# V's main weights: one transfer, or four in the order in which they are multiplied

## The chip, the cores and the metric

The kernel runs on one core of a Trainium2 chip. The metric is the time of one execution in microseconds of device time. Below, TensorE is the matrix engine (PE in the profile, PEld its weight loads), VectorE is DVE, ScalarE is ACT, GpSimd is POOL, and SyncE is SP, which here only issues transfers; SPq and ACTq are the queues of transfers that SP and ScalarE issue.

## The reference

The input x has 2048 rows of 576. It is normalised (layernorm), and two branches read the result: attention with 32 heads of 18 and a sliding window of 256, and a gated MLP with 4608 hidden units. Their outputs are added to x.

```python
def reference(A_x, A_wqkv, A_wo, B_x, B_w1, B_w3, B_w2):
    x = A_x                                   # 1 x 2048 x 576
    xn = _layernorm(x, axis=-1)
    return x + _A_ref(xn, A_wqkv, A_wo) + _B_ref(xn, B_w1, B_w3, B_w2)

def _A_ref(x, wqkv, wo):                      # H = 32, Dh = 18, W = 256
    q, k, v = ((x @ wqkv).reshape(B, S, 3, H, Dh)).transpose(2, 0, 3, 1, 4)
    scores = q k^T * Dh ** -0.5, masked to 0 <= i - j < W
    return softmax(scores) v, heads side by side, @ wo

def _B_ref(x, w1, w3, w2):
    return (silu(x @ w1) * (x @ w3)) @ w2
```

All tensors are bfloat16. The columns 1152 to 1727 of `wqkv` are V's weights: 576 rows, 576 columns.

## The kernel before

**The work.** The 2048 rows are taken in four chunks of 512 (`NC`, `CH`), each of four tiles of 128 rows (`TB`). For each chunk the kernel computes Q, K and V, then the MLP's hidden units with the attention between them, then the output. The normalised rows lie transposed in `xnT`, with the 576 inputs on the partitions: four blocks `kd` of 128 and a last one of 64, which stands on both halves of the partitions.

**Two halves of the array.** Almost every multiplication uses 64 of the 128 rows of the array (`tile_position`), and two run side by side: one on partitions 0 to 63, one on partitions 64 to 127. A projection is cut into two parts (`proj_part`). In part 0 the upper half of the partitions gives column half 0 and the lower half column half 1; in part 1 it is the other way round, so that each output is the sum over all rows. For V a column half is `HD` = 288 columns wide. So V's part 0 reads, of the tile `wv`, partitions 0 to 63 in columns 0 to 287 and partitions 64 to 127 in columns 288 to 575; part 1 reads the rest, and the block `kd` = 4 as well, which is loaded on its own (key `wvd`, line 901).

**The order.** Every operation is added by hand to one list, with the engine that runs it and the keys that it reads and writes. From the keys the program derives the waits: a reader of a loaded tile waits until that load's semaphore has reached the count of its writers. Each engine runs its operations in the order in which they were added. Transfers are added to SP's list or to ScalarE's, and are issued in that order.

**The start.** ScalarE's queue loads x tiles 1 to 3, and SP's queue x tile 0. Behind it SP issues `wv` (line 897, one transfer of four blocks to 128 partitions), `wvd` (901, two), and the weights of Q and K into a staging area that is laid over the tile `pt` (927 and 931, six transfers, semaphores `wqk0`, `wqkd`, `wqk1`). Then come the first six transfers of the MLP's weights (`load_part`, 330), which wait for the second tile's copy of `xnT`. TensorE runs fillers (921, 909, 915) until x tile 0 is normalised; it transposes it (429), ScalarE copies it to `xnT` (442, 448), and V's part 0 of tile 0 starts (500). V's tiles follow as x tiles 1 to 3 become ready; ScalarE and VectorE move V's results to `va` (549, 551). GpSimd and VectorE deal the weights of Q and K from `pt` to `wp` (952, `deal`), and Q's projection (500 with `wp`) comes behind V's last tile. SP then issues `xnS` (463), a copy of `xnT` with the halves of the partitions swapped, which the MLP's first layer (768) reads beside `xnT`.

```python
        early = kind == "v" and c == 0
        order = range(4 + part if kind == "v" else 5 - part)
        for n in order:
            for r in range(2):
                x = r ^ part
                kd, r0 = (4 if n == 4 else n), 64 * r
```

Of the kernel before, what the change touches and what calls it, by code (L numbers as in the profile page):

```python
# [44 lines left out]
class _Prog:  # L45
# [13 lines left out]
    def add(self, eng, fn, r=(), w=(), j=(), dma=None, after=()):  # L59
        deps = []  # L60
        for k in r:
            deps += self.bufs[k].writers
        for k in w:
            g = self.bufs.get(k)
            if g is not None:
                deps += g.ahead(eng)
        for k in j:
            g = self.bufs[k].before
            if g is not None:
                deps += g.ahead(eng)  # L70
        op = _Op(eng, fn, deps + list(after), dma)
        op.after = tuple(after)
        self.n[eng] += 1
        op.pos = self.n[eng]
        if dma is not None:
            self.dma_count[dma] = self.dma_count.get(dma, 0) + 16
            op.cnt = self.dma_count[dma]
        for k in r:
            self.bufs[k].readers.append(op)
        for k in w:  # L80
            self.bufs[k] = _Gen([op], self.bufs.get(k))
        for k in j:
            self.bufs[k].writers.append(op)
        for k in w:
            if self.bufs[k].before is not None:
                self.bufs[k].before.before = None
        self.ops.append(op)
        return op
# [76 lines left out]
def bass_parallel_sum__sliding_block__glu_gated_swiglu__prompt_kernel(  # L165
# [11 lines left out]
    D = A_x.shape[2]  # L177
# [11 lines left out]
    HD = D // 2  # L189
# [6 lines left out]
    add = P.add  # L196

    with ExitStack() as es:

        def sb(name, shape, dtype=dt.bfloat16):  # L200
            return es.enter_context(nc.sbuf_tensor(name, shape, dtype))
# [14 lines left out]
        xnT = sb("xnT", [128, 2, 5, CH])  # L216
        xnS = sb("xnS", [128, 4, CH])
        wv = sb("wv", [128, 5, D])
# [248 lines left out]
        def xk(c):  # L467
            return [("xnT", c % 2, tt) for tt in range(TB)]


        def pair_of(c, i):

            return (((0, 1), (2, 3), (8, 4), (5, 6)) if c == 0 else ((8, 0), (1, 2), (3, 4), (5, 6)))[i]

        def proj_part(c, what, banks, part, behind=()):

            kind, i = what
            last = []
# [6 lines that stand above are left out]
                    rows = slice(r0, r0 + 64)  # L485
                    out_ = PS[:, banks[x], :]
                    if kind == "q":
                        t = pair_of(c, i)[x]
                        st, mv = wp[rows, kd, t, :], xnT[rows, c % 2, kd, :]
                        keys = [("wp", t)] + xk(c)  # L490
                    elif kind == "8":
                        out_ = PS[:, banks[x], 0:CH // 2]
                        st, mv = wp[rows, kd, i, :], xnT[rows, c % 2, kd, x * (CH // 2):(x + 1) * (CH // 2)]
                        keys = [("wp", i)] + xk(c)
                    else:
                        out_ = PS[:, banks[x], 0:HD]
                        st, mv = xnT[rows, c % 2, kd, i * 128:(i + 1) * 128], wv[rows, kd, x * HD:(x + 1) * HD]
                        keys = ["wvd" if kd == 4 else "wv", (("xnTb" if kd // 2 else "xnTa"), i) if early and kd < 4 else ("xnT", c % 2, i)]
                    first = part == 0 and n == 0
                    op = add("pe", lambda e, out_=out_, st=st, mv=mv, n=n, r0=r0, first=first: e.matmul(  # L500
                        out_, st, mv, start=first, stop=(part == 1 and n == order[-1]), tile_position=(r0, 0)),
                        r=keys, after=behind if n == 0 else (), **{"w" if first else "j": [("ps", banks[x])]})
                    if n == order[-1]:
                        last.append(op)
            return last
# [23 lines left out]
        def proj_end(later=None, late=None):  # L529
            if pend:  # L530
                c, what, banks, last = pend.pop()
                proj_part(c, what, banks, 1, last)
                proj_out(c, what, banks, later, late)
                return what

        def proj_begin(c, what, banks=None):
            banks = banks or job()
            last = proj_part(c, what, banks, 0)
            got = proj_end()
            pend.append((c, what, banks, last))  # L540
            return got
# [348 lines left out]
                    p2_mm(ACC[half][tt] if turn is None or turn >= 0 else ACC[0][turn + 2], half, r, *args)  # L890


        xslot = {}
        for t in range(TB):
            xslot[t] = load_x(t, "act" if t else "sp")
        add("act", lambda e: e.preload_act_table_set("sqrt_and_others"))
        add("sp", lambda e: e.dma_start(
            wv[:, 0:4, :], A_wqkv[0:512, 2 * D:3 * D].rearrange("(kd p) f -> p kd f", p=128)),
            w=["wv"], dma="wv")
        for p in range(2):  # L900
            add("sp", lambda e, p=p: e.dma_start(
                wv[64 * p:64 * p + 64, 4, (1 - p) * HD:(2 - p) * HD],
# [21 lines left out]
        for h in range(2):  # L924
            for n in range(2):
# [3 lines left out]
                    dma=f"wqk{h}", **{"j" if n else "w": [f"wqk{h}"]})  # L929
# [119 lines left out]
        for c in range(NC):  # L1049
# [21 lines left out]
            early = [("h", n) for n in range(4 if c == 0 else 0, NHP)]  # L1071
# [111 lines left out]
            for u in range(NF):  # L1183
# [44 lines left out]
                if c == 0 and u == 13:  # L1228
                    for t in range(4):
# [3 lines left out]
                            dma="wo", **{"j" if t else "w": ["wo"]})  # L1233
                if c == 0 and u == 18:
                    rows = A_wo[0:4 * Dh, :].rearrange("(n d) f -> n d f", d=Dh)
                    add("sp", lambda e: e.dma_start(wo[126:128, 0:4, :], rows[:, 0:2, :].rearrange("n d f -> d n f")),
                        j=["wo"], dma="wo")
                    for p in range(2):
                        add("sp", lambda e, p=p: e.dma_start(wo[64 * p:64 * p + 64, 4, :], rows[:, 2:Dh, :]),
                            j=["wo"], dma="wo")  # L1240
# [64 lines left out]
```

## Time and profile before

| | us |
|---|---|
| median of 3 runs | 555.67 (555.06 to 555.78) |
| the profiled execution | 555.25 |
| its span in the profile | 553.5 |
| TensorE busy | 549.7 (99%) |
| VectorE / ScalarE / GpSimd busy | 313.3 / 259.3 / 210.8 |
| HBM read and written | 71.29 MB and 2.36 MB |

The span runs from the first instruction to the last; the 1.75 us between span and time lie around it. A row of the timeline gives the start in us from the span's start, the time taken by the group, the engine, the line of the kernel, the operation, the tile written and the tiles read, and the number of instructions; in brackets stands the idle time of the engine before it and what ended it. For a transfer the time taken is that of its issue on the queue's engine; the DMA view gives the time from issue to landing, and over a window the number of packets, the megabytes and the mean rate. A row of the chain of waits gives a start, a duration, and the work that the end waited for in that stretch.

### The profile page before, as it was taken

What the parts mean: (1) busy time and instruction counts of PE and PEld (TensorE: products, weight loads), DVE (VectorE), ACT (ScalarE), POOL (GpSimd) and SP (SyncE); (2) the same over time, 40 slices, a digit from 0 to 9 for tenths busy, and PEclk for the clock granted to TensorE, in tenths of its full rate; (3) what the DMA queues carried; (4) which work ended last, traced back from release to release, by engine and by line L of the source; (5) the groups of instructions that cost most, each with busy time, mean ns of one, the idle gap of its engine ahead of it and who ended that gap; (6) DMA issues with size and microseconds to landing.
All of it is one profiled execution on the core that took longest, in us unless ns stands there. A gap on an engine that the chain in (4) does not pass through costs nothing.

```text
span 553.5 us, 18356 instructions
## 1 busy us (share of the span) xinstructions
PE 549.7 (99%) x8072; PEld 338.6 (61%) x8072; DVE 313.3 (57%) x587; ACT 259.3 (47%) x365; POOL 210.8 (38%) x380
## 2 busy tenths in 40 slices
PE   8999999999999999999999999999999999999998
PEld 5677544777555544477765454557776545445776
DVE  7476797710468886651056988655105567866311
ACT  7457776000288567700037857760005784775000
POOL 4324675400047456530005745643001553663100
DMA  9997799476577953756746885466673773541750
GB/s 246 204 199 173 199 202 229 129 202 181 141 144 145 188 134 92 186 141 194 185 111 140 173 157 146 124 143 164 183 181 85 139 172 102 152 117 44 194 151 23
DMA packets 128038, 86.00 MB, mean 155 GB/s; under 512 B 35702, under 2 KB 125646, under 8 KB 127958
## 3 DMA queue, kind: packets, MB, share of 16 engines
q1 hardware_dynamic: 89138, 62.80, 49.9%
q10 hardware_dynamic: 38820, 22.02, 15.7%
q8 instruction: 63, 1.03, 0.8%
q14 instruction: 17, 0.14, 0.1%
HBM read 71.29 MB, written 2.36 MB: 133 GB/s over the span
## 4 chain that ended last, share of the span: by engine, by line
PE 99%; DMA 1%; DVE 0%; issue 0%; ACT 0%
PE ps L768 51%; PE ps L839 29%; PE ps L500 10%; PE ps L630 6%; PE ps L698 3%; DMA xp<-in_A_x_dram 1%; PE ps L429 0%; DVE stats L396 0%; DVE xn L414 0%; ACT sd L369 0%; DVE ofin L861 0%; PE ps L915 0%; DVE mv L399 0%; DVE rstd L374 0%
## 5 line engine op out<-in xcount | busy, mean ns | idle before, releaser
L768 PE MATMUL ps<-xnT,w 64*128 64x512 bf16 x1400 | 186.4, 376 | 0.0
L768 PE MATMUL ps<-xnS,w 64*128 64x512 bf16 x1120 | 152.4, 376 | 0.0
L839 PE MATMUL ps<-w,hT 64*128 64x288 bf16 x2292 | 143.7, 282 | 0.0
L783 DVE SCALAR_TENSOR_TENSOR gs<-th,ps 128x512 bf16<-128x512 bf16 x144 | 97.9, 680 | 78.8 <-ACT th L777 78.0
L839 PEld LDWEIGHTS ps<-w,hT 64*128 64x128 bf16 x2292 | 112.3, 94 | 29.5 <-issue 0.2
L777 ACT ACTIVATE th<-ps 128x512 bf16<-128x512 f32 x144 | 85.6, 594 | 60.6 <-PE ps L768 59.7
L768 PEld LDWEIGHTS ps<-xnT,w 64*128 64x128 bf16 x1400 | 69.8, 94 | 61.6
L786 DVE SCALAR_TENSOR_TENSOR hT<-gs,ps 128x512 bf16<-128x512 bf16 x144 | 98.9, 687 | 5.0
L667 POOL TENSOR_TENSOR pt<-pt,mk 128x256 bf16<-128x256 bf16 (+1 forms) x143 | 85.6, 623 | 25.7 <-ACT pt L639 25.7
L639 ACT ACTIVATE pt<-ps 128x1024 bf16<-128x1024 f32 (+1 forms) x80 | 80.8, 1010 | 24.6 <-PE ps L630 24.1
L667 POOL TENSOR_TENSOR hT<-hT,mk 128x256 bf16<-128x256 bf16 (+1 forms) x52 | 30.3, 604 | 160.5 <-ACT hT L639 160.5
L768 PEld LDWEIGHTS ps<-xnS,w 64*128 64x128 bf16 x1120 | 55.6, 94 | 49.0
L513 ACT ACTIVATE stage<-ps 128x512 bf16<-128x512 f32 x16 | 9.6, 597 | 139.4 <-PE ps L500 139.4
L870 DVE TENSOR_TENSOR ofin<-ps,xp 128x288 bf16<-128x288 f32 x31 | 12.2, 451 | 98.5 <-PE ps L839 98.5
L630 PE MATMUL ps<-qv,kv 64*128 64x320 bf16 (+4 forms) x528 | 51.9, 260 | 0.0
L630 PEld LDWEIGHTS ps<-qv,kv 64*128 64x128 bf16 x528 | 26.8, 94 | 28.1 <-ACT pt L639 1.7
L500 PE MATMUL ps<-xnT,wp 64*128 64x512 bf16 (+1 forms) x360 | 38.4, 355 | 0.0
L731 DVE STREAM_TRANSPOSE od<-oq 128x256 bf16<-128x256 bf16 x64 | 25.4, 425 | 12.1 <-POOL oq L724 12.1
L639 ACT ACTIVATE hT<-ps 128x1024 bf16<-128x1024 f32 (+1 forms) x28 | 28.4, 1015 | 7.6 <-PE ps L630 7.4
L667 POOL TENSOR_TENSOR stage<-stage,mk 128x256 bf16<-128x256 bf16 (+1 forms) x44 | 24.8, 586 | 14.2 <-ACT stage L639 14.2
L639 ACT ACTIVATE stage<-ps 128x1024 bf16<-128x1024 f32 (+1 forms) x24 | 24.3, 1014 | 6.9 <-PE ps L630 6.8
L500 PEld LDWEIGHTS ps<-xnT,wp 64*128 64x128 bf16 x360 | 18.3, 94 | 14.5 <-ACT stage L513 0.2
(94 smaller groups left out, 395.9 us busy)
## 6 DMA issues: line engine op xcount, KB each, us to landing
w<-in_B_w_dram SPq DMA_DIRECT2D x210, 192.0 KB, 4.2
w<-in_B_w_dram ACTq DMA_DIRECT2D x70, 288.0 KB, 3.6
xp<-in_A_x_dram SPq DMA_DIRECT2D x29, 144.0 KB, 4.2
out_dram<-ofin SPq DMA_DIRECT2D x31, 72.0 KB, 1.7
xnS<-xnT SPq DMA_DIRECT2D x8, 256.0 KB, 4.7
oT<-od SPq DMA_DIRECT2D x56, 36.0 KB
pt<-in_A_wqkv_dram SPq DMA_DIRECT2D x4, 288.0 KB, 5.3
hT<-in_B_w_dram SPq DMA_DIRECT2D x6, 192.0 KB, 7.4
```

Of the source, the lines that this page charges most:

```text
L500: op = add("pe", lambda e, out_=out_, st=st, mv=mv, n=n, r0=r0, first=first: e.matmul(out_, st, mv, start=first, stop=(part == 1 and n == ...
L630: add("pe", lambda e, r0=r0, out_=out_, kb=kb, q0=q0, nb=nb: e.matmul(out_, kb4[r0:r0 + 64, g, kb + NV - NB, :] if kb < 0 else kv[r0:r0 + ...
L639: add("act", lambda e: e.activation(pt_slot(sl)[:, :, 0:w], PS[:, SC[0]:SC[1] + 1, 0:w], ACT.Exp, scale=scale), r=[("ps", b) for b in SC], ...
L667: add("pool", lambda e, vb=vb, mm=mm: e.tensor_tensor(vb, vb, mm, ALU.mult), r=(key if n == 0 else []) + ["mk"], **{"w" if n == 0 else "j" ...
L698: add("pe", lambda e, p=p, q=q, pr=pr, sl=sl, g=g, pos=pos, q0=q0, nb=nb, col=col, first=first, n=n: e.matmul(PS[32 * q:32 * q + VW, banks ...
L731: add("dve", lambda e: e.transpose(od[i][:, g % 2, c0:c0 + CH // 2], oq[:, c0:c0 + CH // 2]), r=["oq", "oq0"], **{"j" if half or g % 2 els ...
L768: op = add("pe", lambda e, n=n, r0=r0, r=r, k=k, src=src: e.matmul(PS[:, b0 + r, :], wt[r0:r0 + 64, k, fl * 128:(fl + 1) * 128], src, star ...
L777: add("act", lambda e: e.activation(th[i][:], PS[:, bg, :], ACT.Tanh, scale=0.5), r=[("ps", bg)], w=[("th", i)])
L783: add("dve", lambda e: e.scalar_tensor_tensor(out=gs[i][:], in0=th[i][:], scalar=1.0, in1=PS[:, bg, :], op0=ALU.add, op1=ALU.mult), r=[("t ...
L786: add("dve", lambda e: e.scalar_tensor_tensor(out=hT[:, u, :], in0=gs[i][:], scalar=0.5, in1=PS[:, bu, :], op0=ALU.mult, op1=ALU.mult), r= ...
L839: op = add("pe", lambda e: e.matmul(PS[:, bank, 0:w], stat, move, start=new, stop=False, skip_group_check=True, **tile), r=keys, after=hel ...
L870: add("dve", lambda e: e.tensor_tensor(ofin[:, o, :], PS[:, bank, 0:HD], xp[xs[n]][:, d0:d0 + HD], ALU.add), r=[("ps", bank), ("xp", xs[n] ...
```

## The change

The one transfer of `wv`'s four blocks (128 partitions, four runs of 1,152 bytes each) becomes four transfers (64 partitions, four runs of 576 bytes each), all on SP's queue at the same place. The first two carry the rows and columns that V's part 0 multiplies and count on a semaphore `wv0`; the next two carry the rest, for part 1, on a semaphore `wv1`. V's multiplications wait for the semaphore of their part. The block `kd` = 4 keeps its two transfers and its semaphore. The bytes loaded are the same, and so are all multiplications and their order.

```diff
-                        keys = ["wvd" if kd == 4 else "wv", ...]
+                        keys = ["wvd" if kd == 4 else f"wv{part}", ...]
...
+        def load_wv(part, eng):
+            for p in range(2):
+                x = p ^ part
+                add(eng, lambda e, p=p, x=x: e.dma_start(
+                    wv[64 * p:64 * p + 64, 0:4, x * HD:(x + 1) * HD],
+                    A_wqkv[0:512, 2 * D + x * HD:2 * D + (x + 1) * HD].rearrange("(kd q p) f -> q p kd f", q=2, p=64)[p, :, :, :]),
+                    dma=f"wv{part}", **{"j" if p else "w": [f"wv{part}"]})
...
-        add("sp", lambda e: e.dma_start(
-            wv[:, 0:4, :], A_wqkv[0:512, 2 * D:3 * D].rearrange("(kd p) f -> p kd f", p=128)),
-            w=["wv"], dma="wv")
+        load_wv(0, "sp")
+        load_wv(1, "sp")
```

More of the change, by code (lines that the diff above doesn't have):

```diff
@@ L497, in proj_part @@
                         st, mv = xnT[rows, c % 2, kd, i * 128:(i + 1) * 128], wv[rows, kd, x * HD:(x + 1) * HD]
-                        keys = ["wvd" if kd == 4 else "wv", (("xnTb" if kd // 2 else "xnTa"), i) if early and kd < 4 else ("xnT", c % 2, i)]
+                        keys = ["wvd" if kd == 4 else f"wv{part}", (("xnTb" if kd // 2 else "xnTa"), i) if early and kd < 4 else ("xnT", c % 2, i)]
                     first = part == 0 and n == 0
```

## The prediction

> **What bounds the kernel now.** I read the page first (busy times, the shares of the chain), then the chain of waits over the first 24 us, since the change touches only a load that is issued once, then the timeline of each engine around the readers of that load and of the loads behind it, and last the DMA view over short windows for the rates.
>
> ```profile
> span 553.5 us, 18356 instructions
> ...
> PE 549.7 (99%) x8072; PEld 338.6 (61%) x8072; DVE 313.3 (57%) x587; ACT 259.3 (47%) x365; POOL 210.8 (38%) x380
> ...
> PE 99%; DMA 1%; DVE 0%; issue 0%; ACT 0%
> ```
> ```profile
> 0.79 2.78 DMA xp<-in_A_x_dram
> ...
> 5.69 0.41 PE ps L429 x10
> 6.10 0.27 PE ps L915 x6
> 6.38 0.11 issue
> 6.49 0.67 PE ps L500 x8
> ```
>
> TensorE is busy 549.7 of 553.5 us, and the chain that ended last is 99% TensorE; the 1% of DMA is the load of x at the start. So the end moves only by what stops TensorE, and a stop early on is carried to the end, since the work behind it has no idle time on this chain to give back. The chain of the start runs from the landing of the first x tile through the layernorm and the transposes (L429) and fillers (L915) to V's first multiplication at 6.49 (L500). V's weights are not a link of it. The rows around that place, from the timeline, and the landing times of the tile wv:
>
> ```profile
> 5.98 0.37 ACT L442 ACTIVATE xnT<-ps 128x256 bf16<-128x256 bf16 x1
> 6.46 0.39 PEld L500 LDWEIGHTS ps<-wv,xnT 64*128 64x128 bf16 x8 [0.31 <-issue]
> 7.21 0.48 PEld L500 LDWEIGHTS ps<-wv,xnT 64*128 64x128 bf16 x10
> 8.00 0.11 PEld L500 LDWEIGHTS ps<-wv,xnT 64*128 64x128 bf16 x4 [0.30 <-ACT xnT L442]
> 8.27 0.12 PEld L500 LDWEIGHTS ps<-wv,xnT 64*128 64x128 bf16 x4 [0.16 <-ACT xnT L442]
> 8.61 0.32 PEld L429 LDWEIGHTS ps<-ident,xn 64*128 64x128 bf16 x10 [0.22 <-DVE xn L414]
> ```
> ```profile
> wv<-in_A_wqkv_dram SPq DMA_DIRECT2D x1, 576.0 KB, 4.5
> ```
> ```profile
> DMA to landing us min/median/max: 4.4/4.5/4.8
> ```
> ```profile
> 1.25 0.42 SPq L897 DMA_DIRECT2D wv<-in_A_wqkv_dram  x1
> 1.71 1.20 SPq L901 DMA_DIRECT2D wv<-in_A_wqkv_dram  x2
> 2.95 1.14 SPq L927 DMA_DIRECT2D pt<-in_A_wqkv_dram  x2
> 4.13 1.16 SPq L931 DMA_DIRECT2D pt<-in_A_wqkv_dram  x2
> 5.33 1.14 SPq L927 DMA_DIRECT2D pt<-in_A_wqkv_dram  x2
> ```
>
> The main load of wv is issued at 1.25 and lands 4.5 us later, at 5.75. V's first part starts at 6.46, right after ScalarE's copy of xnT, which ends at 5.98 + 0.37 = 6.35. V's weights have waited 0.7 us for their reader.
>
> **The change part by part.** *First half earlier.* Half of wv will land before 5.75. Its reader waits for xnT until 6.35 and starts 0.11 later, so the gain is 0.00. Its upper bound is the 0.11 of issue in the chain, if that were a wait for wv; I take 0, as 5.75 lies 0.6 before the copy's end.
>
> *Three more issues on SP's queue.* SP issues a whole-tile load in 0.46 (1.25 to 1.71) and a load to 64 partitions in 0.62 (1.71 to 2.95 for two). Four of these take 2.48 in place of 0.46, so all that stands behind on SP is issued 2.02 us later: the two transfers of V's last 64 rows (L901, semaphore wvd), the six for Q and K (L927, L931: tile pt), and then the MLP's first weights.
>
> ```profile
> DMA to landing us min/median/max: 4.5/5.3/6.0
> ```
> ```profile
> 8.25 4.90 SPq L330 DMA_DIRECT2D w<-in_B_w_dram  x6
> ```
>
> The first of these two rows is the tile pt: its loads land 4.5 to 6.0 us after their issue, while the first x tile, with nothing ahead of it, needed 2.78 (the chain's first row). What lies between is queueing. The load whose reader is closest is the second of L931, issued about 4.7; 2.02 later plus 2.78 is 9.5 us, before the 10.0 (4.7 plus the median 5.3) at which it lands now. So the later issue is covered by the queue, as long as the 16 engines have a backlog. If that cover were gone, the full 2.02 less the slacks below would be paid. The MLP's loads begin at 8.25 behind ScalarE's copy; SP will be free at 6.47 + 2.02 = 8.49, 0.24 later, also covered by the backlog.
>
> *A slower transfer.* The same 0.59 MB now goes in 1,024 pieces of 576 B instead of 512 of 1,152 B, and each transfer writes only 64 partitions. Three stretches in the DMA view bear on it: 3.75 to 5.25 us (wv beside x: 1,152 B, 128 partitions), 5.75 to 7.25 (mostly L927: 576 B, 128 partitions), and 12.1 to 13.2 (the MLP's weights: 1,024 B, 64 partitions):
>
> ```profile
> DMA packets 532, 0.58 MB, mean 388 GB/s; under 512 B 27, under 2 KB 532, under 8 KB 532
> ```
> ```profile
> DMA packets 859, 0.48 MB, mean 318 GB/s; under 512 B 31, under 2 KB 859, under 8 KB 859
> ```
> ```profile
> DMA packets 262, 0.25 MB, mean 227 GB/s; under 512 B 18, under 2 KB 262, under 8 KB 262
> ```
> ```profile
> DMA packets 212, 0.14 MB, mean 353 GB/s; under 512 B 32, under 2 KB 212, under 8 KB 212
> ```
>
> The fourth is 5.35 to 5.75, V's last rows (576 B, 64 partitions) beside the last x tile: there the engines kept 353 GB/s. Now wv costs 0.59 / 388 = 1.52 us of all engines. Bounds for after: by the piece size alone 0.59 / 318 = 1.86 (0.34 more); by both penalties multiplied, 227 x 318 / 388 = 186 GB/s, 3.17 us (1.65 more). I take the nearest rows: about 0.15 MB of wv passes beside 0.29 MB of x (two tiles of 144 KB, packet for packet) at 353 instead of 388, 0.44 x (1/353 - 1/388) = 0.11 us; the other 0.44 MB goes at 227 instead of 388, 0.81 us. Together all transfers behind wv land **0.92 us** later.
>
> On the 64 partitions the Trainium skill has a rule that speaks against the edit: "SBUF — State Buffer", section "Door 1: The DMA port swizzle", says that partitions 0 to 63, like 64 to 127, reach only 8 of 16 ports, with an asymptote of about 218 GB/s against 436. The trace's 227 against 388 agrees. By the page's 218 the sum would be an estimated 0.59 x (1/218 - 1/388) = 1.19 us in place of 0.92.
>
> *Who meets the delay.* V's second half has until 7.21, wv having landed by 5.75 + 0.92 = 6.67. V's last rows, issued second at 1.71 + 0.62 = 2.33, land at about 2.33 + 4.4 (the least of the tile's times) = 6.73 now and 7.65 then; their reader is the last pair of the ten from 7.21, about 7.6. TensorE may stop 0.2 there, and once more for the added wait of a second semaphore (between 0 and the 0.11 of one issue gap). Behind it stand V's next pairs and the transposes of x tile 2, which idle 0.30, 0.16 and 0.22 anyway for ScalarE and VectorE: 0.68 that covers it. Next is the projection of Q and K, whose weights are dealt from pt into wp:
>
> ```profile
> 10.13 0.84 POOL L952 COPY wp<-pt 128x360 f32<-128x360 f32 x2 [6.14 <-DMA pt<-in_A_wqkv_dram]
> ```
> ```profile
> 10.75 0.23 DVE L952 COPY wp<-pt 128x45 f32<-128x45 f32 x1
> ```
> ```profile
> 10.97 0.40 ACT L549 ACTIVATE va<-ps 64x288 bf16<-64x288 f32 x1
> ```
> ```profile
> 10.99 0.36 PEld L500 LDWEIGHTS ps<-wv,xnT 64*128 64x128 bf16 x8
> 11.48 0.36 PEld L500 LDWEIGHTS ps<-xnT,wp 64*128 64x128 bf16 x6
> ```
>
> GpSimd waits for the DMA until 10.13 and has dealt the first two tiles at 10.97; VectorE's share is done at 10.98. The first weights of Q are loaded at 11.48, 0.11 after ScalarE's evacuation of V frees their banks at 10.97 + 0.40 = 11.37. The deal could end 11.37 - 10.97 = 0.40 later at no cost. With 0.92 it ends at 11.89 and Q's weights load at 12.00: TensorE stops **0.92 - 0.40 = 0.52 us**. VectorE's share may also be reached late, with V's casts queued behind it; their banks are taken by the next projections, which have moved by 0.52 as well. The next reader of a queued transfer is xnS:
>
> ```profile
> DMA to landing us min/median/max: 6.4/6.6/6.8
> ```
> ```profile
> 13.27 1.17 SPq L463 DMA_DIRECT2D xnS<-xnT  x2
> ```
> ```profile
> 21.52 0.81 PEld L768 LDWEIGHTS ps<-xnS,w 64*128 64x128 bf16 x8
> ```
>
> Its second copy is issued about 13.85 and lands 6.8 later, at 20.65, for 21.52. With 0.92 it lands at 21.57, and the reader now stands at 22.04: still in time, and for any larger delay too, since reader and load move together beyond the first 0.40.
>
> Sum: 0 for V, 0 for SP's issues, 0.52 at Q, 0 behind. The profiled execution took 555.25 us (span 553.5, 1.75 around it) and would take 555.77. The median of the runs shown is 555.67, 0.42 above it, so I forecast 555.67 + 0.52 = 556.2: slower by 0.09%, under the 0.2% (1.1 us) that a measurement of this kernel can tell from no change.
>
> **The rivals.** *No cost: the transfers are not slower, or not by more than 0.40.* By piece size alone the delay is 0.34, under the slack, and the time stays 555.7. For it: the 353 GB/s of the short mixed stretch, and the two halves of wv may overlap. Against it: the 227 GB/s, in a stretch where transfers to the two halves of the partitions also alternate. This end is also the one for "not slower". The Trainium skill's "DMA: Bandwidth & Descriptors", section "Specifications", asks only for 512 B or more per transfer for line rate; by that alone 576 B would cost nothing. The trace's 318 against 388 disagrees, at least with wv's stretch. Chance 0.22.
>
> *Slower beyond 0.2%: small pieces and half the partitions add up.* At 186 GB/s for all of wv the delay is 1.65, the stop at Q 1.25, the time 556.9; each 0.1 us for which SP's later issues leave the queue empty adds 0.1. It decides from a delay of 0.40 + 1.11 = 1.51. For it: nothing in the trace shows both penalties sustained, so nothing excludes it. Against it: x runs beside the first part. Chance 0.24.
>
> *Faster: V or the layernorm starts earlier.* If the x tiles land sooner beside smaller pieces, the chain's first link of 2.78 shrinks. To pass 0.2% it would need 1.1 of these 2.78; the first x tile is ahead of wv on the same queue, so a few hundredths are likelier, 555.6 at best beside the stop at Q. That the first half of wv helps is excluded by the 0.7 us it waits already. Chance 0.04.
>
> **How the numbers follow.** The forecast (0.2 to 0.9 slower) has 0.50, the others 0.22, 0.24 and 0.04. The range goes from 555.4 (no cost, less the spread of the runs shown) to 557.2 (both penalties and 0.3 us of an empty queue). The forecast and the no-cost case lie within 0.2%: 0.72 together, of which I give 0.01 to the slower side for a reader further on that I did not follow: faster 0.04, same 0.71, slower 0.25.
>
> **What would show it.** Right: the first two of four wv issues land before 5.75 and V still starts at about 6.46; GpSimd's deal starts near 11.05 instead of 10.13; a gap of about half a microsecond on TensorE before Q's first weights, released by GpSimd; everything from there shifted by the same amount. The DMA view between 4 and 6.7 us would show a mean well under 388 GB/s. Wrong: a deal that still starts before 10.5 (then the no-cost rival holds), a deal after 11.6 or a stop of over 0.7 us in V (then both penalties are real), a start of V before 6.3, or a new wait for a DMA after 21 us.

## The result, and the profile after

| | before | after |
|---|---|---|
| median | 555.53 us (16 runs) | 557.37 us (16 runs) |
| ratio, 95% interval | | 1.0037 [1.0023, 1.0051] |
| the profiled execution | 555.25 us | 557.43 us |

The change makes the kernel 1.84 us slower. The forecast was 556.2 with a range up to 557.2: the direction of its sum was right, its size was not, and the result lies 0.17 above the range. "Within 0.2%" had 0.71 and "slower" 0.25.

Where the time goes shows in three views of the profile after. The page first:

```profile
span 555.7 us, 18360 instructions
...
PE 550.7 (99%) x8072; PEld 331.2 (60%) x8072; DVE 313.3 (56%) x587; ACT 259.4 (47%) x365; POOL 211.3 (38%) x380
...
PE 97%; SPq 1%; DMA 1%; POOL 0%; issue 0%; DVE 0%
```

TensorE is busy 1.0 us longer and the span is 2.2 longer: for the other 1.2 TensorE stands still. The chain that ended last has got a new head, SP's queue and a transfer. The chain of waits over the first 24 us (start, length, what):

```profile
1.25 0.77 SPq L896
2.06 0.62 SPq L896
2.72 0.62 SPq L896
3.38 0.62 SPq L896
4.03 0.61 SPq L908
...
7.71 0.60 SPq L934
...
8.35 6.82 DMA pt<-in_A_wqkv_dram
...
15.22 1.67 POOL wp L959 x3
...
16.93 5.79 PE ps L500 x57
```

In the profile before, this chain ran through x, the layernorm and V. Now it runs through SP's issues, the last load of Q's and K's weights, GpSimd's dealing, and the third projection. That load takes 6.82 us from its issue, where the slowest of the tile took 6.0 before. The timeline of after around V and Q (idle time of the engine and what ended it in brackets):

```profile
6.84 0.36 PEld L500 LDWEIGHTS ps<-wv,xnT 64*128 64x128 bf16 x8 [0.76 <-DMA wv<-in_A_wqkv_dram]
7.79 0.97 PEld L500 LDWEIGHTS ps<-wv,xnT 64*128 64x128 bf16 x18 [0.25 <-DMA wv<-in_A_wqkv_dram]
...
11.39 1.87 POOL L959 COPY wp<-pt 128x360 f32<-128x360 f32 x5 [7.39 <-DMA pt<-in_A_wqkv_dram]
12.30 0.79 PEld L500 LDWEIGHTS ps<-xnT,wp 64*128 64x128 bf16 x10 [0.78 <-DVE wp L959]
...
15.22 1.66 POOL L959 COPY wp<-pt 128x180 f32<-128x180 f32 x3 [1.95 <-DMA pt<-in_A_wqkv_dram]
16.92 5.51 PEld L500 LDWEIGHTS ps<-xnT,wp 64*128 64x128 bf16 x60 [1.08 <-POOL wp L959]
...
22.35 0.09 PEld L768 LDWEIGHTS ps<-xnT,w 64*128 64x128 bf16 x1
```

There are three stops. V starts at 6.84 instead of 6.46, and its second part waits again. Q's first weights load at 12.30 instead of 11.48. At 16.92 there is a third stop of 1.08: GpSimd's eight copies are broken after five, and the last three wait 1.95 for `wqk1`. Before, the eight were one run:

```profile
10.13 3.55 POOL L952 COPY wp<-pt 128x360 f32<-128x360 f32 x8 [6.14 <-DMA pt<-in_A_wqkv_dram]
```

The MLP's first weights load at 22.35; before, they loaded at this row:

```profile
20.77 0.71 PEld L768 LDWEIGHTS ps<-xnT,w 64*128 64x128 bf16 x8
```

That is 1.58 us of the loss within the first 22 us. Of the 0.60 behind it in this execution 0.38 is a stop of TensorE at 193 us, which the waits put to "issue" at L698 and which before does not have; 0.2 is not traced. The medians differ by less than the two executions (1.84 and 2.18).

### The profile page after: what moved, and what is told of

Same layout as the page of the kernel before. It is cut to its first block, busy times and chain, and to the rows that moved or that the text cites. A ratio compares the mean times of both kernels' runs of the same rounds, so it can differ in the third digit from the quotient of the medians.

```text
span 555.7 us, 18360 instructions
## 1 busy us (share of the span) xinstructions
PE 550.7 (99%) x8072; PEld 331.2 (60%) x8072; DVE 313.3 (56%) x587; ACT 259.4 (47%) x365; POOL 211.3 (38%) x380
## 4 chain that ended last, share of the span: by engine, by line
PE 97%; SPq 1%; DMA 1%; POOL 0%; issue 0%; DVE 0%
PE ps L768 51%; PE ps L839 29%; PE ps L500 8%; PE ps L630 6%; PE ps L698 3%; DMA pt<-in_A_wqkv_dram 1%; SPq L896 0%; SPq L934 0%; POOL wp L959 0%; SPq L908 0%; SPq L938 0%; SPq L306 0%; DVE ofin L861 0%
## 5 line engine op out<-in xcount | busy, mean ns | idle before, releaser
L768 PE MATMUL ps<-xnT,w 64*128 64x512 bf16 x1400 | 188.2, 376 | 0.0
L768 PE MATMUL ps<-xnS,w 64*128 64x512 bf16 x1120 | 154.1, 376 | 0.0
L768 PEld LDWEIGHTS ps<-xnT,w 64*128 64x128 bf16 x1400 | 67.5, 94 | 65.5
L768 PEld LDWEIGHTS ps<-xnS,w 64*128 64x128 bf16 x1120 | 53.9, 94 | 52.0
L870 DVE TENSOR_TENSOR ofin<-ps,xp 128x288 bf16<-128x288 f32 x31 | 12.2, 450 | 98.5 <-PE ps L839 98.5
L630 PE MATMUL ps<-qv,kv 64*128 64x320 bf16 (+4 forms) x528 | 53.1, 260 | 0.0
L731 DVE STREAM_TRANSPOSE od<-oq 128x256 bf16<-128x256 bf16 x64 | 25.4, 425 | 12.2 <-POOL oq L724 12.2
```

The source lines that it names most:

```text
L630: add("pe", lambda e, r0=r0, out_=out_, kb=kb, q0=q0, nb=nb: e.matmul(out_, kb4[r0:r0 + 64, g, kb + NV - NB, :] if kb < 0 else kv[r0:r0 + ...
L731: add("dve", lambda e: e.transpose(od[i][:, g % 2, c0:c0 + CH // 2], oq[:, c0:c0 + CH // 2]), r=["oq", "oq0"], **{"j" if half or g % 2 els ...
L768: op = add("pe", lambda e, n=n, r0=r0, r=r, k=k, src=src: e.matmul(PS[:, b0 + r, :], wt[r0:r0 + 64, k, fl * 128:(fl + 1) * 128], src, star ...
L870: add("dve", lambda e: e.tensor_tensor(ofin[:, o, :], PS[:, bank, 0:HD], xp[xs[n]][:, d0:d0 + HD], ALU.add), r=[("ps", bank), ("xp", xs[n] ...
```

## The experiments

Three explanations stood at the start: transfers to 64 partitions are slower; pieces of 576 B are slower; issuing later costs by itself, because the queue runs dry. All ratios are against the kernel before, run beside each kernel on the same chip.

**Cutting `wv` in four along one axis only.** `kd4` cuts by input block (128 partitions, pieces of 1,152 B), `col4` by column half and pair of blocks (128 partitions, 576 B), `half4` by partition half and pair of blocks (64 partitions, 1,152 B). All keep one semaphore.

```diff
 # kd4
+ for kd in range(4): ... wv[:, kd, :], A_wqkv[128 * kd:128 * kd + 128, 2 * D:3 * D]
 # col4: k = 2 * (n // 2), x = n % 2
+ for n in range(4): ... wv[:, k:k + 2, x * HD:(x + 1) * HD], ...
 # half4: k = 2 * (n // 2), p = n % 2
+ for n in range(4): ... wv[64 * p:64 * p + 64, k:k + 2, :], ...
```

> V's main weights in four transfers by input block: 128 partitions, pieces of 1,152 B, one semaphore. Only the number of issues is as in the changed kernel. If writing to 64 partitions (A) or the small pieces (B) cost the time: 555.5, as before, wv landing near 5.8, GpSimd's deal at 10.1. If the later issues on SP's queue (C) cost it: the weights of Q and K are issued about 1.4 later instead of 2.0, so about 1.4/2.0 of the 1.84 us, 556.8.

> Four transfers by column half and pair of blocks: 128 partitions, pieces of 576 B, one semaphore. A (64 partitions): 555.5, deal at most 0.4 later. B (pieces): 557.3, wv landing after 6.5. C (issues, 2.0 us later): 557.3 with wv landing near 6.

> Four transfers by partition half and pair of blocks: 64 partitions, pieces of 1,152 B, one semaphore. A: 557.3 or more, since now V's first part needs all four, with wv landing near 7.7 and the transfers ending far apart. B: 555.5. C: 557.3 with wv landing near 6.

Measured: `kd4` 1.0019 [1.0011, 1.0028], `col4` 1.0028 [1.0014, 1.0042], `half4` 1.0036 [1.0023, 1.0049]. V's first row in the three profiles:

```profile
6.89 0.36 PEld L500 LDWEIGHTS ps<-wv,xnT 64*128 64x128 bf16 x8 [0.83 <-DMA wv<-in_A_wqkv_dram]
```
```profile
6.45 0.39 PEld L500 LDWEIGHTS ps<-wv,xnT 64*128 64x128 bf16 x8 [0.31 <-DMA wv<-in_A_wqkv_dram]
```
```profile
7.66 0.36 PEld L500 LDWEIGHTS ps<-wv,xnT 64*128 64x128 bf16 x8 [1.45 <-DMA wv<-in_A_wqkv_dram]
```

With pieces of 576 B on all partitions (`col4`) `wv` is there in time; in pieces of 1,152 B on half the partitions (`half4`) V starts 1.2 us later. Piece size costs nothing that shows here. The 1.2 is not all the price of half the partitions: the fourth transfer is issued at 3.34 in `half4`, at 2.73 in `col4` and at 2.65 in `kd4`, and in `kd4`, with all partitions, V starts 0.43 later than in before. The next two runs separate this better. And `kd4` and `col4` cost time, `col4` without a late V: its loss is a stop at the third projection of 1.2 us, as in after.

```profile
16.28 5.51 PEld L500 LDWEIGHTS ps<-xnT,wp 64*128 64x128 bf16 x60 [1.22 <-POOL wp L955]
```

Something besides the form of the pieces was at work.

**Two transfers instead of four.** `kd2` and `half2` add one issue only; `kd2` cuts by blocks, `half2` by partition halves.

```diff
 # kd2
+ for n in range(2): ... wv[:, 2 * n:2 * n + 2, :], A_wqkv[256 * n:256 * n + 256, 2 * D:3 * D]...
 # half2
+ for p in range(2): ... wv[64 * p:64 * p + 64, 0:4, :], ...
```

> wv in two transfers of two input blocks each, 128 partitions and 1,152 B; the issues behind come 0.45 later. The partner of half2 with whole partitions. A and C: 555.5 to 555.8, wv landing near 5.8.

> wv in two transfers by partition half, 64 partitions and 1,152 B; the issues behind come 0.8 later. A: wv lands after 6.6 instead of 5.75 and V starts late, 556.5 or more. C alone: 0.8/2.0 of the loss at most, 556.0 or less, wv landing near 5.8.

Measured: `kd2` 1.0000 [0.9991, 1.0009], `half2` 1.0047 [1.0031, 1.0063]. The waits of TensorE's weight loads over the first 40 us (total, times, longest), `kd2` and then `half2`:

```profile
PEld ps L500 <- DMA wv<-in_A_wqkv_dram: 0.9, 1, 0.9
```
```profile
PEld ps L500 <- DMA wv<-in_A_wqkv_dram: 2.0, 1, 2.0
```

With half the partitions per transfer V waits 2.0 instead of 0.9 and starts at 8.36 instead of 7.04; there is no stop at Q behind this one. Of the 1.32, 0.34 is the second transfer's later issue (2.05 and 1.71). The rates from 3 to 8 us (the last two figures: the packets' time as a share of the engines', and GB/s), again `kd2` and then `half2`:

```profile
3.00:8.00 5.00, 4.37 (x83) 3.42 (x82) 4.20 (x15) 4.10 (x13) 0.99 (x2) 1.00 1.09 348
```
```profile
3.00:8.00 5.00, 3.74 (x61) 2.75 (x58) 4.16 (x14) 3.92 (x12) 0.99 (x2) 1.00 1.03 251
```

The engines are busy in both and move 251 GB/s in place of 348, with the same piece size, so the half partitions are shown as a cost. The 0.47% is more than this cost: eight of the twelve executions of `half2` had a granted clock of 0.994 or 0.997. The four at 1.000 have a median of 556.74, 1.0 us above the 555.73 of before. The Trainium skill's "SBUF — State Buffer", section "Door 1: The DMA port swizzle", says that either half reaches 8 of 16 ports. The lower rate agrees; ports are not seen in these runs.

**The late issues by themselves.** `issue3` leaves `wv` as it was and puts three loads of 64 x 32 B into an unused tile behind it. `late` adds nothing: the two transfers of L901 wait for VectorE's clearing of another tile, so that everything behind `wv` on SP is issued about 1.65 us later.

```diff
 # issue3
+ for n in range(3):
+     add("sp", lambda e, n=n: e.dma_start(junk[:, n, :], A_wqkv[0:64, 16 * n:16 * n + 16]), dma="junk", ...)
 # late (the clearing of qv moved in front)
-     ... dma="wvd", **{"j" if p else "w": ["wvd"]})
+     ... r=[("q", 0)], dma="wvd", **{"j" if p else "w": ["wvd"]})
```

> The kernel before with three transfers of 64 x 32 B to an unused tile issued on SP's queue right behind wv: the issues of the weights of Q and K are 1.9 us later as in the changed kernel, wv itself is untouched. A and B: 555.5. C: 557.2, V starting at 6.46 and the deal about 1.2 late.

> The kernel before, in which V's last rows wait for VectorE's clearing of qv, which ends near 3.3: all of SP's issues behind wv come about 1.6 us later, with no transfer added, split or moved. If the lateness of the issues (C) costs the time: V starts at 6.46 as before, GpSimd's deal starts about 1 us late, 556.6 to 557.0. If only the form of wv's transfers costs it (A, 64 partitions): 555.5.

Measured: `issue3` 1.0046 [1.0029, 1.0064] (its median 558.12, its profiled execution 560.69, so only the order of events is read from that), `late` 1.0013 [1.0003, 1.0024]. `issue3` did not leave `wv` alone as it should have: V starts at 7.20 and waits 0.95 for it. In `late` V starts on time and Q stops; the timelines' rows, and the second a stretch of 1 us with the mean rate at its end (PE, PEld, DVE, ACT, POOL busy, clock, DMA share, GB/s), of `late` and of before:

```profile
12.02 1.86 POOL L952 COPY wp<-pt 128x360 f32<-128x360 f32 x5 [8.02 <-DMA pt<-in_A_wqkv_dram]
12.93 0.79 PEld L500 LDWEIGHTS ps<-xnT,wp 64*128 64x128 bf16 x10 [1.62 <-DVE wp L952]
```
```profile
6.00:7.00 1.00, 0.89 (x20) 0.60 (x14) 0.96 (x4) 0.98 (x5) 0.00 (x0) 1.00 0.75 173
```
```profile
6.00:7.00 1.00, 0.89 (x18) 0.59 (x17) 0.96 (x4) 0.99 (x5) 0.00 (x0) 1.00 1.15 308
```

The deal begins 1.9 us later for 1.65 us of lateness, and at 6 to 7 us the packets take a share of 0.75 of the engines' time instead of 1.15 and the rate is 173 GB/s instead of 308: the queue runs short. I took this for the proof that lateness is paid in full. It was not the whole story, as the last seven runs show.

**Order, semaphores, queues, neighbours.** `onesem` is the changed kernel with one semaphore. `twoq` is `half2` with the upper half on ScalarE's queue, `pool1` is the changed kernel with its second pair on GpSimd's queue, `gate` the changed kernel with the first six loads of the MLP's weights issued behind `xnS`, so that they don't run beside those of Q and K.

```diff
 # onesem
-     dma=f"wv{part}", ...
+     dma="wv", **{"j" if p or part else "w": ["wv"]})
 # twoq
+ if t == 1: add("act", ... wv[64:128, 0:4, :], ... dma="wv1", w=["wvh"])
 # pool1
-        load_wv(1, "sp")
+        load_wv(1, "pool")
 # gate
-        load_w13([("xnTb", 1)])
...
         xn_swap(0, ("sp", "sp"))
+        load_w13()
```

> The changed kernel with one semaphore for all four transfers: V's first part waits for the second pair too, near 7.75 instead of 6.8. If V's start sets the end, 558.3; if the weights of Q and K, which land as in the changed kernel, set it: 557.4, as the changed kernel.

> The two transfers of half2, but the lower half of the partitions (64 to 127) is issued on ScalarE's queue behind x tile 1, so that both halves are written at the same time. ScalarE's own work starts about 0.4 later for it, and the issues behind wv on SP come 0.3 later. If 64 partitions take only half the rate while the other half stands still (A): both transfers land before 6.3, V starts within 0.5 of 6.46, 555.6 to 556.2. If a transfer to 64 partitions is slow whatever runs beside it: one of them lands after 7.5, 557 or more.

> The changed kernel with the second pair (V's part 1) issued on GpSimd's queue: SP's issues behind wv come 0.8 later instead of 2.0, the transfers keep their form. C: the deal starts before 10.9 and about half of the loss comes back, 556.3 to 556.8. A alone: 557.4 as the changed kernel, V's first wait unchanged.

> The changed kernel with the first six loads of the MLP's weights issued behind xnS, about 3.5 us later. In the changed kernel's profile the last weights of Q and K landed 6.8 us after their issue, at 15.2, and TensorE stopped 0.6 for them. If the MLP's loads beside them hold them up: they land before 13.8, the second stop goes, 556.8. If not: they land at 14.5 or later, 557.4 or, with the MLP's weights late for their reader, more.

Measured: `onesem` 1.0036 [1.0023, 1.0049], `twoq` 1.0051 [1.0033, 1.0069], `pool1` 1.0044 [1.0028, 1.0059], `gate` 1.0045 [1.0028, 1.0061]. The second semaphore brings nothing that the time shows, though V starts at 6.84 with it and at 7.60 in `onesem`. `twoq` decides nothing: the transfer in front of ScalarE's first work made that start about 1 us late. `pool1` starts V at 7.73, so another queue does not bring the halves in earlier. `gate` does not bear out the idea that the MLP's loads slow those of Q and K: without them its deal is later still. It is no clean test, since the packet described next came at 8.9 in it and at 10.0 in after.

```profile
12.82 3.46 POOL L959 COPY wp<-pt 128x360 f32<-128x360 f32 x8 [8.81 <-DMA pt<-in_A_wqkv_dram]
```

**What holds up one engine.** In after, `late`, `col4` and `onesem`, fifteen of the sixteen engines have finished a load of Q and K 1.4 to 1.6 us before the last one, by the landings in the trace (1.2 in `gate`, 1.9 in `issue3`); in after 13.5 against 15.2 for `wqk1`. In before the last engine is at most 0.04 behind. The DMA view has one candidate: a queue of its own, "q8 instruction". On before's page (packets, MB, share), and then in the stretches 10.9 to 12.2 us of before, 9 to 10.5 of `late`, 10 to 11.4 of after:

```profile
q8 instruction: 63, 1.03, 0.8%
```
```profile
q8 instruction: 1, 0.02, 5.7%
```
```profile
q8 instruction: 1, 0.02, 5.3%
```
```profile
q8 instruction: 1, 0.02, 5.5%
```

63 packets of 16 KB, and 2 x 8,072 weight loads and matmuls: one packet holds about 256 instructions, if all are TensorE's. One packet is 5.3% of 16 engines for 1.5 us, that is 1.3 us of one engine (1.2 in the other two). In before it falls at 10.9, where the last load has slack; in `late` at 9.1 and in after at 10.0, among loads that are waited for. In `half2`, `twoq` and `pool1` it comes at 12.6 to 12.7, and there the last engine is at most 0.4 behind on these loads. To move it without touching a transfer, four kernels change the fillers that TensorE runs before x lands, at the same 5,120 columns: 10 matmuls of 512 in place of 55 (`fill_late` on `late`, `fill_after` on the changed kernel, `fill_before` on before), or 80 of 64 (`fill_more`, on before).

```diff
-        for k, n in enumerate([CH] * 3 + [128] * 4 + [64] * 48):
+        for k, n in enumerate([CH] * 10):      # fill_more: [64] * 80
```

> The kernel before with the late issues of L901 (all loads behind wv about 1.65 us later), and with TensorE's fillers at the start in 10 matmuls of 512 columns instead of 55 of 512, 128 and 64: the same 5,120 columns in 45 matmuls fewer. If a fetch of TensorE's instructions, 16 KB on one data engine beside the loads of Q and K, is what makes one engine's share land 1.5 us after the others, the fetch comes later with fewer instructions, all of wqkd lands by 10.5, GpSimd's first deal starts before 11.0 and the time is within 0.4 us of the kernel before. If only the queue and its late issues decide, the deal stays near 12.0, the stop at Q near 1.3 us and the time 1.0 to 1.3 us above the kernel before.

> The changed kernel with the same 10 fillers. If the fetch is part of its loss (the second stop, at the third projection, with one engine's share of wqk1 landing at 15.2 against 13.5 for the others): that stop shrinks from 1.08 to under 0.3 us, and the ratio comes down from 1.0037 to about 1.002. If not: 1.003 to 1.004, and the stop stays.

> The kernel before with the same 10 fillers: in it the loads of Q and K land in time, so the fetch costs nothing and the time stays within 0.3 us (either theory). A time more than 0.5 us lower would mean that a fetch costs something in the kernel before too.

> The kernel before, nothing changed in its loads, with the fillers cut into 80 matmuls of 64 columns (the same 5,120 columns, 25 matmuls more). If the fetch beside the loads is a cost of its own: it now falls at about 9.5 us in place of 10.9, one engine's share of the loads of Q and K is late, GpSimd's deal starts 0.5 to 1.5 us later than 10.13 and the time is 0.3 to 1.0 us above the kernel before. If only the lateness of the issues decides: no change within 0.3 us.

The times missed every expectation: `fill_late` 1.02 [1.0172, 1.0229], `fill_after` 1.0188 [1.0163, 1.0213], `fill_before` 1.0168 [1.0146, 1.019], `fill_more` 1.0195 [1.0162, 1.0229], some 10 us for 45 matmuls fewer or 25 more (8 to 10 in the six executions at a granted clock of 1.000; the others had 0.994 or 0.997). But the first 22 us of the profiles answer the question. GpSimd's deal in `fill_late`, with the MLP's first load, and in `fill_after`:

```profile
10.46 3.45 POOL L952 COPY wp<-pt 128x360 f32<-128x360 f32 x8 [6.47 <-DMA pt<-in_A_wqkv_dram]
...
20.72 0.66 PEld L768 LDWEIGHTS ps<-xnT,w 64*128 64x128 bf16 x8
```
```profile
11.39 3.61 POOL L959 COPY wp<-pt 128x360 f32<-128x360 f32 x8 [7.40 <-DMA pt<-in_A_wqkv_dram]
...
21.58 0.65 PEld L768 LDWEIGHTS ps<-xnT,w 64*128 64x128 bf16 x8
```

In `fill_late` everything behind `wv` is still issued 1.65 us late, but the deal starts at 10.46 (12.02 in `late`, 10.13 in before), nothing stops, and the MLP begins at 20.72, 0.05 earlier than in before. In `late` it began 1.44 later than in before:

```profile
22.21 0.65 PEld L768 LDWEIGHTS ps<-xnT,w 64*128 64x128 bf16 x8
```

In `fill_after` the eight copies are one run again and the third stop is gone; the first two stay, and the MLP begins at 21.58: 0.81 after before, 0.67 after `fill_before` (20.91). `fill_more` did not do what it was made for: its packet came at 10.7, not at 9.5, and its deal was on time (9.85). So no run has put the packet among the loads of the kernel before.

The 10 us are seen in the waits further on. TensorE's waits for "issue" in `fill_before` and in before:

```profile
PEld ps L698 <- issue: 13.0, 15, 3.6
```
```profile
PEld ps L698 <- issue: 3.8, 9, 0.4
```

The two longest stops of `fill_before` contain an instruction packet each (191.96 to 193.31, 332.77 to 334.13):

```profile
194.67 0.08 PEld L698 LDWEIGHTS ps<-stage,va 64*20 64x20 bf16 x1 [3.00 <-issue]
```
```profile
335.49 0.12 PEld L698 LDWEIGHTS ps<-pt,va 64*20 64x20 bf16 x12 [3.60 <-issue]
```

As far as the times tell, TensorE stands there in L698's row of short multiplications and waits for its own program: where 90 instructions are missing at the start, the program's blocks end at other places, and some of these lie in that row. In `fill_more` the stops lie at L768 (11.1 us in all).

**The same with the blocks put back.** The 45 matmuls that the new fillers take away come back as 16 by 16 multiplications in front of the MLP's first, behind the packet in question, so that the program from there on stands where it stood.

```diff
+                    if c == 0 and u == 0 and n == 0 and r == 0:
+                        for k_ in range(45):
+                            add("pe", lambda e: e.matmul(PS[0:16, b0, 0:16], ones[:, 0:16], ones[:, 0:16], start=True, stop=True), ...)
```

> The kernel before with 10 start fillers in place of 55, and the 45 matmuls that this takes away put back in a small form (16 by 16) in front of the MLP's first multiplication, so that all of TensorE's program behind them stands where it stood. If the 10 us of the four kernels with other fillers came from the place of the program's blocks, they are gone and the time is 555.3 plus 1 to 3 us for the 45 small matmuls. If they came from the fillers themselves (fewer or longer ones), the time stays near 565.

> The kernel with the late issues (about 1.65 us, nothing added to the loads) with the same fillers and the same 45 small matmuls as comp_before; comp_before is its measure. If late issues cost only through the fetch of TensorE's instructions that falls among the loads of Q and K, this one is within 0.4 us of comp_before. If lateness costs by itself: 1.0 to 1.4 us above comp_before.

> The changed kernel with the same fillers and small matmuls; comp_before is its measure. If the fetch makes the second of its stops (at the third projection) and the slower transfers the others: 0.7 to 1.1 us above comp_before in place of 1.8 to 2.0. If the fetch has no part in it: 1.8 to 2.0 above.

| | median, us | ratio to before | over comp_before, us |
|---|---|---|---|
| before | 555.67 | | |
| comp_before | 556.83 | 1.0022 [1.0012, 1.0031] | |
| comp_late | 556.75 | 1.0015 [1.0003, 1.0027] | -0.08 |
| comp_after | 557.57 | 1.0030 [1.0017, 1.0043] | +0.74 |

The 10 us are gone, so they came from the blocks' places and not from the fillers. The 45 small matmuls are a row of `comp_before`:

```profile
21.45 1.17 PEld L770 LDWEIGHTS ps<-const-bfloat16-1.0 128*16 128x16 bf16 x45 [0.21 <-issue]
```

With the packet out of the way the late issues cost nothing (-0.08 instead of 1.3 us by the medians), and the change costs 0.74 instead of 1.84. The intervals of `comp_after` and `comp_before` overlap, so 0.74 is no sharp number. The profiles of `fill_after` and `fill_before` give 0.67 for it. Those of `comp_after` and `comp_before` give 0.09 only (the small matmuls start at 21.54 and 21.45). In that execution of `comp_before` one engine is 0.3 to 0.9 us behind the others from x tile 2 to `wqk1`, with no instruction packet before 12.7, and its deal starts at 10.67. So single executions of one kernel may differ at the start by as much as is left to explain. No run is a version that beats the kernel before.

## Why the prediction was right or wrong

**The chain and the place.** Right: the end moves by what stops TensorE early on, and a stop is not given back. The stops at V, at Q and at the third projection make 1.58 of the loss.

**First half earlier, gain 0.** The gain was 0, but the step failed: it expected a landing before 5.75 and V at 6.46. The first half was waited for until V's start at 6.84. Two transfers of a quarter of the bytes, each to half of the partitions, arrive later than all of it in one transfer: by the landings at 6.80, where the one transfer landed at 5.78. Of this 1.02, 0.81 is the second transfer's later issue, at 2.06, which the step left out. The first transfer, issued at 1.25 like the one before, is no earlier than that (its sixteen counts are in at 5.77), though it carries a quarter of the bytes; that half the partitions slow a transfer is what `half2` against `kd2` shows.

**Three more issues, covered by the queue.** The shift was 2.38 (L934 starts at 5.33, L927 started at 2.95) for a forecast of 2.02: the four issues take 2.78 to the next one's start, their first 0.81. The cover held, nearly. The tile pt's times from issue to landing, of `late` and of `fill_late`:

```profile
DMA to landing us min/median/max: 3.6/4.5/7.1
```
```profile
DMA to landing us min/median/max: 3.3/4.0/4.6
```

Before, they were 4.5/5.3/6.0. A load that is issued 1.65 later stands 1.3 less in the queue (4.0 against 5.3); 0.33 is left at the deal, and nothing stops. In `late` the median is short too, but the longest is 7.1, and of `wqkd`, for which Q's deal waits there, fifteen engines are done by 10.5 and the last at 11.9. So the step's rule was good for the queue and had no term for what the later load meets: I looked at the backlog in front of a load and not at what comes beside it.

**A slower transfer, 0.92.** The mechanism was right and the size too small: the deal came at 11.39, 1.26 later than 10.13, the same in `fill_after`, where the packet is away. The sign in the DMA view came as forecast: from 4 to 6.7 us the engines move 254 GB/s, 356 before. The 0.92 and the 0.33 of the step before make 1.25; the forecast had put the 0.33 at nothing. That the sums meet is an argument, not a run, and the 0.33 belongs to issues that are 1.65 late, not 2.38. The bound by piece size (0.34) had nothing in it: `col4` brought `wv` in time with 576 B. Here the Trainium skill's "DMA: Bandwidth & Descriptors", section "Specifications", with its 512 B, was nearer than my reading of 318 against 388 GB/s, which compared two different mixes.

**V covered by 0.68 of idle time.** Half right. V waited 0.76 and 0.25; the idle rows behind it took up most of that.

**A stop of 0.52 at Q.** Right in kind and place, and too small: 0.78, with Q's weights 0.82 later than before.

**Nothing behind.** This term failed, and it is the one that took the result out of the range. I followed the first deal and xnS, not GpSimd's last three copies and the load `wqk1` that they wait for. There lay a stop of 1.08 us. Taking away the packet of instructions took it away (`fill_after`), and of the loss, by the medians, 1.84 - 0.74 = 1.10.

**The rivals.** "Small pieces and half the partitions add up" gave 556.9 and wanted a deal after 11.6 or a stop of over 0.7 in V. The stop came (0.76), but for the half partitions alone. "No cost" and "faster" did not happen. None of them had the mechanism that decided: another transfer on the same engines.

**What stays open.** Why the packet comes at 9.1 in `late` and at 10.9 in before, though TensorE's program is the same and V on time: that it waits behind the backlog of its engine in before, and finds it empty in `late`, fits the rates but wasn't tried. That it lies on the very engine that finishes last is argued from the times, not read from a view. What else can hold up an engine: in `issue3` fifteen have finished `wv` by 5.83 and the last at 7.16, with no instruction packet before 9.75, and `comp_before` has its late engine without one too. `issue3`'s size (1.0046 against 1.0013 for `late`) isn't broken up beyond this.

## What to carry to other kernels

Ask of a load that is moved not only when it is issued and how fast it goes, but what else will use the engines in its new place, and follow every load behind it to its reader: the step that was missing was the last load, not the nearest. Here a transfer to half of the partitions was slower than the same bytes over all of them (251 against 348 GB/s); split along blocks or columns instead, and only if a reader waits, since four transfers in place of one cost 0.19% (`kd4`) and 0.28% (`col4`) even so. A change in the number of TensorE's instructions moves the ends of all its program blocks behind it: put as many back before a comparison, or compare profiles stretch by stretch.

## What the runs showed of the hardware

- **TensorE's program passes through the data engines.** 63 packets of 16 KB per execution, 1.2 to 1.3 us of one engine each; beside loads that are waited for, one of them cost 1.1 to 1.4 us of the kernel by the medians (after and `late`, against their forms with the packet moved). The Trainium skill's "Runtime: NRT & Kernel Launch", section "Instruction fetch mechanics", describes blocks of 256 instructions on a queue of their own, and calls the price of a block's end mostly hidden. Size and queue agree with the trace; the price does not.
- **Where the blocks end can cost 2%.** Ninety instructions fewer at the start cost 10 us (555.3 to 565.4; 8.2 and 9.7 in the two executions at a granted clock of 1.000), in stops of up to 3.6 us; with the instructions put back, 556.8.
- **A landing is the last engine's.** `wqk1` in after: fifteen engines by 13.5 us, the last at 15.2. The same skill's "DMA: Bandwidth & Descriptors", section "Why a DMA increments its semaphore by 16 and not by 1", says that each engine counts when its own share is in; the trace agrees.
- **The engines may run short of work and nothing be lost.** Issues 1.65 us later (173 in place of 308 GB/s for a microsecond in `late`) cost nothing once the packet was away: `comp_late` is 0.08 us under `comp_before`.
